# A fused attention and SwiGLU kernel: input transposed by the loading DMAs, or loaded plainly and turned on TensorE

## The chip, the cores and the metric

The kernel runs on one NeuronCore of a Trainium2 chip. The metric is the device time of one execution in microseconds (us), the median of several runs; before the change it is 844.42 us (three runs, 843.98 to 845.3). The profile shows one execution, whose span is 843.2 us.

The engines named below are TensorE (PE in the profile; its weight loads are PEld), VectorE (DVE), ScalarE (ACT), GpSimd (POOL) and SyncE (SP, which here only issues DMAs). Each runs its own instructions in order and waits on semaphores for the others.

## The reference

```python
x = A_x                                            # 1 x 2048 x 512, bf16
g = sigmoid((x * gate_w).sum(-1, keepdims=True))
qkv = (x @ A_wqkv).reshape(B, S, 3, 32, 16)        # 32 heads of 16
p = softmax(q @ k.T / sqrt(16))                    # 2048 x 2048 for each head
a = (p @ v, heads side by side) @ A_wo
b = (silu(x @ B_w_gate) * (x @ B_w_up)) @ B_w_down # 512 -> 1792 -> 512
out = g * a + (1 - g) * b
```

Every product needs x with its 512 features on the partitions, that is transposed: the tile `xT` of the kernel holds 4 blocks of 128 features (`dc`) by 2048 tokens.

## The kernel before

**The main loop.** Scores are made for a group of four heads (`g`, 8 of them), a quarter of 512 queries (`qb`, 4 of them) and a block of 128 keys. Most blocks get their exponential on ScalarE (tile `e_t`), the others get one that VectorE puts together from integer and float steps (tiles `y_t`, `z_t`, `u_t`, with one addition done by a DMA that GpSimd issues). A planner in the Python code simulates the engines and writes the order of TensorE, ScalarE and VectorE instructions by hand: `mm`, `act` and `vec` chain each instruction to the one before it on its engine (`ordered`, lines 145 to 168; most rows of the profile therefore carry L157, L160 or L166, and are told apart by their tiles). Projections, the FFN and the output products are put between the scores by the same planner. It starts counting after the start-up described next, so its order doesn't depend on it.

**The start-up.** Before the first scores the kernel needs K of head group 0 for all 2048 keys (written to `kaug[:, 0]`), Q of group 0 for the first 512 queries (`q0[0]`), and a bound that is subtracted ahead of the exponential: the largest magnitude of each row of K, times the magnitudes of Q.

- Lines 172 to 174: eight DMAs on SyncE's queue write `xT` through the transposing DMA, first the four feature blocks of the first 1024 tokens, then those of the second. ScalarE's queue loads the first 64 columns of the K, Q and V weights (lines 176 to 183). The remaining weights follow on SyncE's queue.
- Lines 211 to 236: VectorE writes constants, and spreads the K and Q weights of group 0 into zero-padded tiles (`wpad`, line 229), and presets three of the seven other groups of `kaug` with ones (`ones_rows`, line 234), a fourth one later (line 1013). GpSimd presets the last three and other tiles, and makes the identity matrix `ident` after them.
- Lines 992 to 1027: TensorE starts with 14 matmuls on zeros (`keep_warm`), then takes the feature blocks as they come: `k0(dc, tb)` adds one feature block to the K of a quarter of the tokens, in the PSUM tiles `kp0`; the Q of the first quarter goes to `qp0`. Two or three more `keep_warm` matmuls stand between the blocks. `v0` makes V of group 0 for eight token blocks.
- `largest` (a VectorE maximum over `kp0` into `kpart0`), small VectorE steps that turn it into the weights `kneg1` and `kneg0`, `k0_evict` (ScalarE, PSUM to `kaug[:, 0]`), ScalarE's copies of `qp0` to `q0r` and to `aq0` (magnitude), two masked VectorE copies from `q0r` to `q0[0]`, then the bound `bp0` and its addition to `q0[0]` close the start-up.

PSUM has eight banks here: two `kp0` tiles of two banks each (later the score tiles `s_t`), the three banks of `ps_m`, and the one of `ps_o`, where `keep_warm` writes.

Of the kernel before, what the change touches and what calls it, by code (L numbers as in the profile page):

```python
# [8 lines left out]
ACT = mybir.ActivationFunctionType  # L9
ALU = mybir.AluOpType  # L10
AX = mybir.AxisListType
BF16 = mybir.dt.bfloat16
F32 = mybir.dt.float32
# [65 lines left out]
def kernel(  # L79
# [12 lines left out]
    nc = tc.nc  # L92
    P = 128
    x = A_x.flatten_outer_dims()
    S, D = x.shape
    F = B_w_gate.shape[1]
    DH = 16
    H = D // DH
    G = H // 4
    NB = H // 8  # L100
    DC = D // P
    FC = F // P
    KT = S // P
    QBW = 512
    QB = S // QBW
    TQ = QBW // P
# [23 lines left out]
    const = ctx.enter_context(tc.tile_pool(name="const", bufs=1))  # L130
    big = ctx.enter_context(tc.tile_pool(name="big", bufs=1))
    work = ctx.enter_context(tc.tile_pool(name="work", bufs=2))
# [6 lines left out]
    ps_o = ctx.enter_context(tc.tile_pool(name="ps_o", bufs=1, space=bass.MemoryType.PSUM))  # L139
    ps_m = [ctx.enter_context(tc.tile_pool(name=f"ps_m{i}", bufs=1, space=bass.MemoryType.PSUM)) for i in range(3)]  # L140
# [4 lines left out]
    def ordered(ins):  # L145
        i = ins.ins
        if i.engine in last_of:
            tc.add_manual_dep(
                i, last_of[i.engine].name,
                mybir.DependencyInfo(mybir.DependencyClass.NoSync, mybir.DependencyReason.DATA),  # L150
                reason="order",
            )
        last_of[i.engine] = i
        return ins

    def mm(*args, **kw):
        return ordered(nc.tensor.matmul(*args, **kw))  # L157

    def act(*args, **kw):
        ordered(nc.scalar.activation(*args, **kw))  # L160
# [7 lines left out]
    vec = Ordered()  # L168


    xT = big.tile([P, DC, S], BF16, name="xT")
    for t0 in (0, 2 * QBW):
        for dc in range(DC):
            nc.sync.dma_start_transpose(out=xT[:, dc, t0:t0 + 2 * QBW], in_=x[t0:t0 + 2 * QBW, dc * P:(dc + 1) * P])
    wqk = big.tile([P, DC, 2 * D], BF16, name="wqk")
    for c0 in (D, 0):

        nc.scalar.dma_start(out=wqk[:, :, c0:c0 + 64],
                            in_=A_wqkv[:, c0:c0 + 64].rearrange("(dc p) c -> p dc c", p=P))

    rb = big.tile([P, NB, QBW], BF16, name="rb")
    wv = rb[:, :, :]
    nc.scalar.dma_start(out=wv[:, :, 0:64], in_=A_wqkv[:, 2 * D:2 * D + 64].rearrange("(dc p) c -> p dc c", p=P))

    nc.sync.dma_start(out=wv[:, :, 64:D], in_=A_wqkv[:, 2 * D + 64:3 * D].rearrange("(dc p) c -> p dc c", p=P))
    for c0 in (D, 0):
        nc.sync.dma_start(out=wqk[:, :, c0 + 64:c0 + D],
                          in_=A_wqkv[:, c0 + 64:c0 + D].rearrange("(dc p) c -> p dc c", p=P))
# [1 line left out]
    wo_t = big.tile([P, NB, D], BF16, name="wo_t")  # L190

    wo_l = big.tile([P, 2, D], BF16, name="wo_l")
    wd_t = big.tile([P, FC, D], BF16, name="wd_t")

    def late_loads():
        nc.sync.dma_start(out=gw_col[:], in_=gate_w.rearrange("(dc p) -> p dc", p=P))
# [9 lines left out]

    kaug = big.tile([P, G, S], BF16, name="kaug")

    mt = big.tile([P, FC, QBW], BF16, name="mt")
    idle = mt[:, 4, :]  # L210
    nc.vector.memset(idle, 0.0)
    wpad = [mt[:, i, :].rearrange("p (dc c) -> p dc c", c=P) for i in range(2)]
# [7 lines left out]
    vsel = const.tile([P, 2], F32, name="vsel")  # L220
# [3 lines left out]
    bsel0 = mt[:, 3, 0:P]  # L224
    nc.vector.memset(bsel0, 0.0)
    for j in range(4):
        nc.vector.memset(bsel0[32 * j:32 * j + 32, 32 * j:32 * j + 1], -1.0)
    for i in (1, 0):
        nc.vector.tensor_copy(
            out=wpad[i][:, :, :].rearrange("p dc (j c) -> p dc j c", c=32)[:, :, :, 1:1 + DH],  # L230
            in_=wqk[:, :, i * D:i * D + 64].rearrange("p dc (j c) -> p dc j c", c=DH))
    def ones_rows(engine, g):

        engine.memset(kaug[:, g, :].bitcast(F32), 1.0019378662109375)
    for g in range(1, 4):
        ones_rows(nc.vector, g)
    vaug = big.tile([P, KT, G * 4 * VC + 16], BF16, name="vaug")
    nc.gpsimd.memset(vaug[:, :, G * 4 * VC:], 0.0)

# [9 lines left out]
    for h in range(8):  # L249
        c = 2 * (h % 4) + h // 4  # L250
# [9 lines left out]
    nc.gpsimd.memset(sel_t[:], 0.0)  # L260
    for j in range(4):
        nc.gpsimd.memset(sel_t[32 * j:32 * j + 1, j:j + 1], 1.0)
    ident = const.tile([P, P], BF16, name="ident")
    nc.gpsimd.memset(ident[:], 1.0)
    nc.gpsimd.affine_select(out=ident[:], in_=ident[:], pattern=[[-1, P]], compare_op=ALU.is_equal,
                            fill=0.0, base=0, channel_multiplier=1)

    kb = const.tile([P, NB], F32, name="kb")
    kneg = const.tile([P, NB, 8], BF16, name="kneg")
# [74 lines left out]
    def m_free(ps, t):  # L344
        i = [h is ps for h in held].index(True)
        banks[i], held[i] = t + 0.2, None
# [96 lines left out]
    def v0(t0):  # L443

        p = m_tile("vp")
        for i in range(8):
            for dc in range(DC):
                mm(p[:, 64 * i:64 * i + 64], lhsT=xT[:, dc, (t0 + i) * P:(t0 + i + 1) * P], rhs=wv[:, dc, 0:64],
                   start=(dc == 0), stop=(dc == DC - 1))
        act(out=vaug[:, t0:t0 + 8, 0:4 * VC].rearrange("p t (h c) -> p t h c", c=VC)[:, :, :, 1:1 + DH],  # L450
            in_=p[:, :].rearrange("p (t h c) -> p t h c", h=4, c=DH), func=ACT.Copy)
        m_free(p, 0.0)
# [26 lines left out]
    q1 = big.tile([P, 2, QBW], BF16, name="q1")  # L479
    nc.gpsimd.memset(q1[:], 0.0)  # L480
    nc.gpsimd.memset(qx[0][:], 0.0)
    for g in range(5, G):
        ones_rows(nc.gpsimd, g)

    q0 = [(qx[1][:, :, :, :], on_t[0][:, :, :].rearrange("p (v i) q -> p v i q", v=2))[qb // 2][:, :, qb % 2, :]
          for qb in range(QB)]
# [479 lines left out]
    kp0 = [ps_s.tile([P, 2 * QBW], F32, tag="s", name="kp0") for _ in range(2)]  # L966
    qp0 = m_tile("qp0")
# [3 lines left out]
    def keep_warm(n):  # L971
        for _ in range(n):
            mm(warm[:, :], lhsT=idle[:, 0:P], rhs=idle[:, :], start=True, stop=True)

    def k0(dc, tb):
        mm(kp0[tb // 2][:, (tb % 2) * QBW:(tb % 2 + 1) * QBW], lhsT=wpad[1][:, dc, :],
           rhs=xT[:, dc, tb * QBW:(tb + 1) * QBW], start=(dc == 0), stop=(dc == DC - 1))

    kpart0 = const.tile([P, 3], F32, name="kpart0")
    aq0 = work.tile([P, QBW], BF16, tag="aq", name="aq0", bufs=4)  # L980
    q0r = work.tile([P, QBW], BF16, tag="qst", name="q0r")
    kneg0 = mt[:, 3, P:2 * P]
    kneg1 = mt[:, 3, 2 * P:3 * P]

    def largest(i, ps):
        vec.tensor_reduce(out=kpart0[:, i:i + 1], in_=ps, axis=AX.X, op=ALU.max, apply_absolute_value=True)

    def k0_evict(i):
        act(out=kaug[:, 0, i * 2 * QBW:(i + 1) * 2 * QBW], in_=kp0[i][:, :], func=ACT.Identity,
            bias=onescol[:, 0:1], scale=1.0)  # L990

    keep_warm(14)
    for dc in range(DC):
        for tb in range(2):
            k0(dc, tb)
        mm(qp0[:, :], lhsT=wpad[0][:, dc, :], rhs=xT[:, dc, 0:QBW], start=(dc == 0), stop=(dc == DC - 1))
        if dc < DC - 1:
            keep_warm(2)
    largest(0, kp0[0][:, :])
    act(out=q0r[:, :], in_=qp0[:, :], func=ACT.Copy)  # L1000
    act(out=aq0[:, :], in_=qp0[:, :], func=ACT.Abs)
    vec.tensor_scalar(out=kneg1, in0=bsel0, scalar1=kpart0[:, 0:1], scalar2=None, op0=ALU.mult)
    for v in range(2):
        vec.tensor_scalar(out=q0[0][:, v, :], in0=q0r[:, :], scalar1=vsel[:, v:v + 1], scalar2=None, op0=ALU.mult)
    k0_evict(0)
    for dc in range(DC - 1):
        for tb in (2, 3):
            k0(dc, tb)
        if dc == 0:
            v0(0)  # L1010
        else:
            keep_warm(3)
    ones_rows(vec, 4)
    k0(DC - 1, 2)
    largest(1, kp0[1][:, 0:QBW])
    vec.scalar_tensor_tensor(out=kneg0, in0=bsel0, scalar=kpart0[:, 1:2], in1=kneg1, op0=ALU.mult, op1=ALU.min)
    k0(DC - 1, 3)
    largest(2, kp0[1][:, QBW:2 * QBW])
    vec.scalar_tensor_tensor(out=kneg0, in0=bsel0, scalar=kpart0[:, 2:3], in1=kneg0, op0=ALU.mult, op1=ALU.min)
    k0_evict(1)  # L1020
    v0(8)
    bp0 = m_tile("bp0")
# [2 lines left out]
    for v in range(2):  # L1025
        vec.scalar_tensor_tensor(out=q0[0][:, v, :], in0=bp0[:, :], scalar=vsel[:, v:v + 1],
                                 in1=q0[0][:, v, :], op0=ALU.mult, op1=ALU.add)
# [3 lines left out]
                            op0=ALU.is_gt, op1=ALU.mult)  # L1031
    vec.scalar_tensor_tensor(out=bsel[:, :], in0=lo_t[:], scalar=0.5, in1=far_t[:],
                                   op0=ALU.is_lt, op1=ALU.mult)
# [15 lines left out]
    for qb in range(1, QB):  # L1049
        d = qb * KT  # L1050
# [5 lines left out]
    for qb in range(QB):  # L1056
        for b in range(NB):
            d = UNIT.index((qb, max(2 * b, 1))) * KT
# [31 lines left out]
    for qb in range(QB):  # L1090
        a0 = f0 + per * qb
        for fc in range(FC):
            load, pcs = gu[(qb, fc)]
            i = order_.index((qb, fc))
# [10 lines left out]
            c = pace.add(pcs, 58, a0 + per * (0.6 if qb < QB - 1 else 0.68) * (fc + 1) / FC, prev)  # L1105
            prev = [c]
        for tq in range(0, TQ, 2):
            c = pace.add(down_pieces(qb, tq), 0 if qb else 100, a0 + per * (0.6 + 0.3 * (tq + 2) / TQ if qb < QB - 1 else 0.68 + 0.32 * (tq + 2) / TQ), prev + fin_prev + gates)
# [191 lines left out]
    while au < UNITS:  # L1300
# [10 lines left out]
        if room > 0.02:  # L1311
# [6 lines left out]
            c = side(room + SLACK)  # L1318
# [9 lines left out]
            if room > 0.4 and closed in o_of and 0 < pvs[closed] < KT - 1 and sum(  # L1328
                    w for t, w in work_at[-24:] if t > plan.pe - 3.0) < 6.5:

                for j in range(4):
                    mm(o_of[closed][32 * j:32 * j + 16, :], lhsT=vaug[:, 0, G * 4 * VC:], rhs=xT[:, 0, 0:QBW],
                       start=False, stop=False, tile_position=(0, 32 * j), skip_group_check=True)
# [11 lines left out]
    while closed < UNITS or vops or added or vcur:  # L1345
# [9 lines left out]
        c = side(2.0)  # L1355
# [28 lines left out]
    for tq in range(TQ):  # L1384
        for j in range(4):
            mm(rps[32 * j:32 * j + 32, tq * P:(tq + 1) * P],
               lhsT=rt[:, 4 * tq + j:4 * tq + j + 1].broadcast_to([P, 32]), rhs=ident[:, :],
               start=True, stop=True, tile_position=(0, 32 * j), skip_group_check=True)
# [45 lines left out]
```

## Time and profile before

| | before |
|---|---|
| median time | 844.42 us |
| span of the profiled execution | 843.2 us |
| HBM read over the span | 20.83 MB |
| matmuls, `keep_warm` in the start-up | 26 |
| first matmul on `xT` | 6.68 us |
| last matmul of the start-up's K | 15.62 us |
| first exponential of the main loop | 18.83 us |

A row of the profile's timeline has the start in us from the beginning of the span, the duration in us, the engine, the line of the kernel, the operation, the tiles (output <- inputs), the shape, and how many instructions were merged into the row; in brackets stands how long the engine was idle before it and what released it. A row of the groups by shape ends with busy time and the mean duration of one in ns, then the idle time before them and its releasers. The table by stages has the stretch, its length, the busy time of PE, PEld, DVE, ACT and POOL with the number of instructions, the TensorE clock granted, the share of the DMA engines' time, and GB/s.

### The profile page before, as it was taken

To read this page: it belongs to the slowest core of one execution; us is meant where nothing else is said; L and a number is where in the kernel's file an instruction comes from. 1 tells how busy PE (TensorE), PEld (TensorE's weight loads), DVE (VectorE), ACT (ScalarE), POOL (GpSimd) and SP (SyncE) were. 2 spreads that over 40 slices of the span, in tenths; PEclk is the share of its full clock that TensorE was granted. 3 is DMA by queue.
4 is the path that set the end of the run, shared out by engine and by line. 5 is a ranking of instruction groups with operands and counts; after the bars stand their busy time and mean duration, and the time that the engine had idled before them with its cause. 6 is when DMAs were issued, how large, how long until landed. Compare 5 with 4: busy or idle time off the path is not lost. (4 is left out here: it accounts for less than half of the span.)

```text
span 843.2 us, 16224 instructions
## 1 busy us (share of the span) xinstructions
PE 763.7 (91%) x6047; PEld 263.8 (31%) x6076; DVE 795.7 (94%) x1159; ACT 815.1 (97%) x912; POOL 93.2 (11%) x122
## 2 busy tenths in 40 slices
PE   8999998999888998989889988899899898988997
PEld 3222233332332332222223323223333233332332
DVE  5999998999999999999999898999998999999996
ACT  3999999999999999999999999999999999999996
POOL 5010100010011010111010100100100110111000
PEclk9999999999999999999999999999999999999999
DMA  9432445245454334544443354454442464354232
GB/s 204 127 64 51 83 82 113 61 95 110 95 105 96 79 68 105 108 106 99 95 97 81 77 117 87 84 110 93 98 91 55 89 124 96 76 118 97 57 69 51
DMA packets 101416, 78.23 MB, mean 93 GB/s; under 512 B 77761, under 2 KB 89625, under 8 KB 101337
## 3 DMA queue, kind: packets, MB, share of 16 engines
q0 software_dynamic: 12672, 46.14, 28.7%
q1 hardware_dynamic: 86792, 30.60, 15.5%
q8 instruction: 47, 0.77, 0.4%
q10 hardware_dynamic: 1872, 0.46, 0.2%
q14 instruction: 33, 0.26, 0.1%
HBM read 20.83 MB, written 2.34 MB: 27 GB/s over the span
## 5 line engine op out<-in xcount | busy, mean ns | idle before, releaser
L160 ACT ACTIVATE e_t<-s_t 128x1024 bf16<-128x1024 f32 x846 | 791.9, 1103 | 8.2 <-PE s_t L157 6.2
L157 PE MATMUL s_t<-qx,kaug 64*128 64x512 bf16 x1376 | 293.8, 382 | 36.3 <-ACT e_t L160 31.2
L166 DVE TENSOR_SCALAR y_t<-d_t 128x512 uint16<-128x512 f32 x356 | 234.4, 680 | 16.4 <-PE d_t L157 13.5
L157 PEld LDWEIGHTS <-kaug 64*128 64x128 bf16 x2048 | 137.4, 93 | 324.1 <-issue 288.2
L157 PE MATMUL o_ps<-e_t,vaug 128*32 128x512 bf16 x1692 | 159.9, 389 | 1.5 <-DVE osb L166 1.0
L157 PE MATMUL gu_a<-xT,wg 64*128 64x512 bf16 x448 | 135.7, 377 | 0.0
L157 PE MATMUL gu_b<-xT,wu 64*128 64x512 bf16 x448 | 134.6, 377 | 1.2 <-DVE y_t L166 0.9
L157 PE MATMUL d_t<-qx,kaug 64*128 64x512 bf16 x288 | 107.6, 379 | 17.1 <-DVE y_t L166 10.3
L157 PEld LDWEIGHTS <-vaug 128*32 128x32 bf16 (+1 forms) x2132 | 45.6, 93 | 146.1 <-issue 144.8
L778 POOL DMA_DIRECT2D y_t<-u_t x44 | 40.1, 912 | 352.1 <-PE s_t L157 182.3
L778 POOL DMA_DIRECT2D y_t<-kaug x38 | 36.0, 946 | 309.7 <-PE s_t L157 199.7
L157 PE MATMUL dps_b<-wd_t,mt 64*128 64x512 bf16 x224 | 65.0, 375 | 0.3 <-DVE y_t L166 0.2
L157 PE MATMUL dps_a<-wd_t,mt 64*128 64x512 bf16 x224 | 64.9, 376 | 0.0
L166 DVE TENSOR_SCALAR z_t<-y_t 128x2048 uint16<-128x2048 uint16 x89 | 61.4, 690 | 2.1
L166 DVE TENSOR_SCALAR y_t<-y_t 128x2048 uint16<-128x2048 uint16 x89 | 60.8, 683 | 0.7 <-DMA y_t<-kaug 0.5
L166 DVE TENSOR_TENSOR u_t<-u_t 128x2048 f16<-128x2048 f16 x44 | 53.8, 1222 | 1.1
L166 DVE TENSOR_TENSOR u_t<-u_t,z_t 128x2048 f16<-128x2048 f16 x44 | 53.5, 1215 | 0.1
L157 PE MATMUL s_t<-q,kaug 64*128 64x512 bf16 x212 | 43.1, 381 | 7.6 <-ACT e_t L160 7.1
L166 DVE TENSOR_TENSOR kaug<-kaug 128x2048 f16<-128x2048 f16 x39 | 47.7, 1223 | 0.9
L157 PEld LDWEIGHTS <-wg 64*128 64x128 bf16 x448 | 41.3, 94 | 20.0 <-issue 7.7
L166 DVE TENSOR_TENSOR kaug<-kaug,z_t 128x2048 f16<-128x2048 f16 x39 | 47.4, 1216 | 0.1
L157 PEld LDWEIGHTS <-wu 64*128 64x128 bf16 x448 | 41.8, 94 | 14.7 <-issue 0.2
(131 smaller groups left out, 632.5 us busy)
## 6 DMA issues: line engine op xcount, KB each, us to landing
y_t<-u_t POOLq DMA_DIRECT2D x44, 512.0 KB, 4.8
y_t<-kaug POOLq DMA_DIRECT2D x38, 512.0 KB, 4.9
wg<-in_B_w_gate_dram SPq DMA_DIRECT2D x56, 128.0 KB
wu<-in_B_w_up_dram SPq DMA_DIRECT2D x56, 128.0 KB
y_t<-wd_t POOLq DMA_DIRECT2D x6, 512.0 KB, 4.6
on<-osb SPq DMA_DIRECT2D x120, 16.0 KB
rb<-rr SPq DMA_DIRECT2D x15, 128.0 KB
wd_t<-in_B_w_down_dram SPq DMA_DIRECT2D x7, 256.0 KB
```

What stands on the lines that cost most here:

```text
L157: return ordered(nc.tensor.matmul(*args, **kw))
L160: ordered(nc.scalar.activation(*args, **kw))
L166: return lambda *a, **kw: ordered(f(*a, **kw))
L778: nc.gpsimd.dma_start(out=ya, in_=ua, accum_op=ALU.add)
```

## The change

The input is loaded as it lies in HBM, a quarter of 512 tokens by each of four plain DMAs, into places that are free at that time: three quarters of the tile `wd_t` (the down-projection's weights come later) and a part of `mt`. TensorE turns it: a matmul with a 128x128 block of x as the weights and `ident` as the moving operand leaves the transposed block in PSUM. Four of them fill one bank (`tp`), which VectorE or ScalarE copies to `xT` (`turn`). Three banks take turns. The start-up is now ordered by quarters: turn the four feature blocks of the quarter, then its K, then its maximum.

With it go smaller edits. The padding of the weights moves from VectorE to ScalarE (`pad`), all seven presets of `kaug` go to GpSimd, whose identity matrix now comes first. The masked copies to `q0[0]` read `qp0` in PSUM, without `q0r`. The V columns for group 0 are loaded on SyncE's queue, between the second and third quarter of x. `kneg1` takes its minimum with a tile of zeros, in the form of instruction that the later steps have. `keep_warm` is left at the start alone, with 8 matmuls. The purpose is to load the input with plain descriptors, and to keep VectorE from copies within SBUF while GpSimd writes its presets.

```diff
     xT = big.tile([P, DC, S], BF16, name="xT")
-    for t0 in (0, 2 * QBW):
-        for dc in range(DC):
-            nc.sync.dma_start_transpose(out=xT[:, dc, t0:t0 + 2 * QBW], in_=x[t0:t0 + 2 * QBW, dc * P:(dc + 1) * P])
+    wd_t = big.tile([P, FC, D], BF16, name="wd_t")
+    mt = big.tile([P, FC, QBW], BF16, name="mt")
+    x_rows = [wd_t[:, TQ * b:TQ * b + TQ, :] for b in range(QB - 1)] + [mt[:, 8:8 + TQ, :]]
...
+    for b in range(QB):
+        nc.sync.dma_start(out=x_rows[b], in_=x[b * QBW:(b + 1) * QBW, :].rearrange("(i p) d -> p i d", p=P))
+        if b == 1:
+            nc.sync.dma_start(out=wv[:, :, 0:64],
+                              in_=A_wqkv[:, 2 * D:2 * D + 64].rearrange("(dc p) c -> p dc c", p=P))
...
-    for i in (1, 0):
-        nc.vector.tensor_copy(
-            out=wpad[i][:, :, :].rearrange("p dc (j c) -> p dc j c", c=32)[:, :, :, 1:1 + DH],
-            in_=wqk[:, :, i * D:i * D + 64].rearrange("p dc (j c) -> p dc j c", c=DH))
+    def pad(i):
+        act(out=wpad[i][:, :, :].rearrange("p dc (j c) -> p dc j c", c=32)[:, :, :, 1:1 + DH],
+            in_=wqk[:, :, i * D:i * D + 64].rearrange("p dc (j c) -> p dc j c", c=DH), func=ACT.Copy)
+    pad(1)
...
-    for g in range(1, 4):
-        ones_rows(nc.vector, g)
...
-    for g in range(5, G):
+    for g in range(1, G):
         ones_rows(nc.gpsimd, g)
...
-    keep_warm(14)
-    for dc in range(DC):
-        for tb in range(2):
-            k0(dc, tb)
-        mm(qp0[:, :], lhsT=wpad[0][:, dc, :], rhs=xT[:, dc, 0:QBW], start=(dc == 0), stop=(dc == DC - 1))
-        if dc < DC - 1:
-            keep_warm(2)
-    largest(0, kp0[0][:, :])
-    act(out=q0r[:, :], in_=qp0[:, :], func=ACT.Copy)
-    act(out=aq0[:, :], in_=qp0[:, :], func=ACT.Abs)
...
+    def turn(b, dc):
+        i = len(tps) % 3
+        tps.append((ps_m[1].tile([P, QBW], F32, tag="m1", name="tp") if i == 0 else
+                    ps_m[2].tile([P, QBW], F32, tag="m2", name="tp") if i == 1 else
+                    ps_o.tile([P, QBW], F32, tag="o", name="tp")))
+        tp = tps[-1]
+        for k in range(TQ):
+            mm(tp[:, k * P:(k + 1) * P], lhsT=x_rows[b][:, k, dc * P:(dc + 1) * P], rhs=ident[:, :],
+               start=True, stop=True)
+        dst = xT[:, dc, b * QBW:(b + 1) * QBW]
+        if dc % 2 or dc and b in (1, 2):
+            act(out=dst, in_=tp[:, :], func=ACT.Copy)
+        else:
+            vec.tensor_copy(out=dst, in_=tp[:, :])
+
+    keep_warm(8)
+    for b in range(QB):
+        for dc in range(DC):
+            turn(b, dc)
+        if b == 0:
+            pad(0)
+        if b == 2:
+            v0(0)
+        for dc in range(DC):
+            k0(dc, b)
+            if b == 0:
+                mm(qp0[:, :], lhsT=wpad[0][:, dc, :], rhs=xT[:, dc, 0:QBW], start=(dc == 0), stop=(dc == DC - 1))
+        if b == 0:
+            act(out=aq0[:, :], in_=qp0[:, :], func=ACT.Abs)
+            for v in range(2):
+                vec.tensor_scalar(out=q0[0][:, v, :], in0=qp0[:, :], scalar1=vsel[:, v:v + 1], scalar2=None, op0=ALU.mult)
+        elif b == 1:
+            largest(0, kp0[0][:, :])
+            vec.scalar_tensor_tensor(out=kneg1, in0=bsel0, scalar=kpart0[:, 0:1], in1=idle[:, 0:P],
+                                     op0=ALU.mult, op1=ALU.min)
+            k0_evict(0)
         else:
...
+            largest(b - 1, kp0[1][:, (b - 2) * QBW:(b - 1) * QBW])
+            vec.scalar_tensor_tensor(out=kneg0, in0=bsel0, scalar=kpart0[:, b - 1:b], in1=(kneg1, kneg0)[b - 2],
+                                     op0=ALU.mult, op1=ALU.min)
     k0_evict(1)
     v0(8)
```

More of the change, by code (lines that the diff above doesn't have):

```diff
@@ L171 @@
     xT = big.tile([P, DC, S], BF16, name="xT")
-    for t0 in (0, 2 * QBW):
-        for dc in range(DC):
-            nc.sync.dma_start_transpose(out=xT[:, dc, t0:t0 + 2 * QBW], in_=x[t0:t0 + 2 * QBW, dc * P:(dc + 1) * P])
+    wd_t = big.tile([P, FC, D], BF16, name="wd_t")
+    mt = big.tile([P, FC, QBW], BF16, name="mt")
+    x_rows = [wd_t[:, TQ * b:TQ * b + TQ, :] for b in range(QB - 1)] + [mt[:, 8:8 + TQ, :]]
+    rb = big.tile([P, NB, QBW], BF16, name="rb")
+    wv = rb[:, :, :]
+    for b in range(QB):
[3 more added lines that the diff above has]
+                              in_=A_wqkv[:, 2 * D:2 * D + 64].rearrange("(dc p) c -> p dc c", p=P))
     wqk = big.tile([P, DC, 2 * D], BF16, name="wqk")
@@ L179 @@
                             in_=A_wqkv[:, c0:c0 + 64].rearrange("(dc p) c -> p dc c", p=P))
-    rb = big.tile([P, NB, QBW], BF16, name="rb")
-    wv = rb[:, :, :]
-    nc.scalar.dma_start(out=wv[:, :, 0:64], in_=A_wqkv[:, 2 * D:2 * D + 64].rearrange("(dc p) c -> p dc c", p=P))
     nc.sync.dma_start(out=wv[:, :, 64:D], in_=A_wqkv[:, 2 * D + 64:3 * D].rearrange("(dc p) c -> p dc c", p=P))
@@ L192 @@
     wo_l = big.tile([P, 2, D], BF16, name="wo_l")
-    wd_t = big.tile([P, FC, D], BF16, name="wd_t")
     def late_loads():
@@ L207 @@
     kaug = big.tile([P, G, S], BF16, name="kaug")
-    mt = big.tile([P, FC, QBW], BF16, name="mt")
     idle = mt[:, 4, :]
@@ L227 @@
         nc.vector.memset(bsel0[32 * j:32 * j + 32, 32 * j:32 * j + 1], -1.0)
-    for i in (1, 0):
-        nc.vector.tensor_copy(
-            out=wpad[i][:, :, :].rearrange("p dc (j c) -> p dc j c", c=32)[:, :, :, 1:1 + DH],
-            in_=wqk[:, :, i * D:i * D + 64].rearrange("p dc (j c) -> p dc j c", c=DH))
+    def pad(i):
+        act(out=wpad[i][:, :, :].rearrange("p dc (j c) -> p dc j c", c=32)[:, :, :, 1:1 + DH],
+            in_=wqk[:, :, i * D:i * D + 64].rearrange("p dc (j c) -> p dc j c", c=DH), func=ACT.Copy)
+    pad(1)
     def ones_rows(engine, g):
         engine.memset(kaug[:, g, :].bitcast(F32), 1.0019378662109375)
-    for g in range(1, 4):
-        ones_rows(nc.vector, g)
+    ident = const.tile([P, P], BF16, name="ident")
+    nc.gpsimd.memset(ident[:], 1.0)
+    nc.gpsimd.affine_select(out=ident[:], in_=ident[:], pattern=[[-1, P]], compare_op=ALU.is_equal,
+                            fill=0.0, base=0, channel_multiplier=1)
     vaug = big.tile([P, KT, G * 4 * VC + 16], BF16, name="vaug")
@@ L262 @@
         nc.gpsimd.memset(sel_t[32 * j:32 * j + 1, j:j + 1], 1.0)
[L263 to L266, printed above, removed]
     kb = const.tile([P, NB], F32, name="kb")
@@ L980 @@
     aq0 = work.tile([P, QBW], BF16, tag="aq", name="aq0", bufs=4)
-    q0r = work.tile([P, QBW], BF16, tag="qst", name="q0r")
     kneg0 = mt[:, 3, P:2 * P]
@@ L990, in k0_evict @@
             bias=onescol[:, 0:1], scale=1.0)
-    keep_warm(14)
-    for dc in range(DC):
-        for tb in range(2):
-            k0(dc, tb)
-        mm(qp0[:, :], lhsT=wpad[0][:, dc, :], rhs=xT[:, dc, 0:QBW], start=(dc == 0), stop=(dc == DC - 1))
-        if dc < DC - 1:
-            keep_warm(2)
-    largest(0, kp0[0][:, :])
-    act(out=q0r[:, :], in_=qp0[:, :], func=ACT.Copy)
-    act(out=aq0[:, :], in_=qp0[:, :], func=ACT.Abs)
-    vec.tensor_scalar(out=kneg1, in0=bsel0, scalar1=kpart0[:, 0:1], scalar2=None, op0=ALU.mult)
@@ L1003 @@
[L1003 to L1009, printed above, removed]
-            v0(0)
-        else:
[L1012 to L1016, printed above, removed]
@@ L1017 @@
-    k0(DC - 1, 3)
-    largest(2, kp0[1][:, QBW:2 * QBW])
-    vec.scalar_tensor_tensor(out=kneg0, in0=bsel0, scalar=kpart0[:, 2:3], in1=kneg0, op0=ALU.mult, op1=ALU.min)
+    tps = []
+    def turn(b, dc):
[12 more added lines that the diff above has]
+            vec.tensor_copy(out=dst, in_=tp[:, :])
```

## The prediction

> **What bounds the kernel now.** I read the page first: parts 1 and 5 say that ScalarE's exponentials fill the span.
>
> ```profile
> PE 763.7 (91%) x6047; PEld 263.8 (31%) x6076; DVE 795.7 (94%) x1159; ACT 815.1 (97%) x912; POOL 93.2 (11%) x122
> ...
> L160 ACT ACTIVATE e_t<-s_t 128x1024 bf16<-128x1024 f32 x846 | 791.9, 1103 | 8.2 <-PE s_t L157 6.2
> ```
>
> 846 exponentials keep ScalarE busy; it idles only 8.2 us before them. So the time is the moment of the first exponential plus a stretch that hardly has holes. The change works ahead of that moment only: comparing the lists of instructions of the two built programs, with names stripped of their numbers, every engine has the same order after the first scores. The question is therefore when the first exponential starts. The timeline of the first 24 us answers for before:
>
> ```profile
> 0.81 11.24 SPq L174 DMA_TRANSPOSE xT<-in_A_x_dram  x8
> ...
> 14.46 0.38 PE L157 MATMUL kp<-xT,mt 128*128 128x512 bf16 x1
> ...
> 14.88 0.69 DVE L166 TENSOR_REDUCE kpart<-kp 128x1 f32<-128x512 f32 x1 [1.22 <-PE kp L157]
> ...
> 16.03 0.69 DVE L166 TENSOR_REDUCE kpart<-kp 128x1 f32<-128x512 f32 x1
> 16.76 1.11 ACT L160 ACTIVATE kaug<-kp,onescol 128x1024 bf16<-128x1024 f32 x1 [3.35 <-DVE kpart L166]
> ...
> 17.77 0.59 ACT L160 ACTIVATE vaug<-vp 128x512 bf16<-128x512 f32 x1
> ...
> 18.83 2.98 ACT L160 ACTIVATE e_t<-s_t 128x1024 bf16<-128x1024 f32 x3 [0.47 <-PE s_t L157]
> ...
> 23.34 13.36 ACT L160 ACTIVATE e_t<-s_t 128x1024 bf16<-128x1024 f32 x14 [1.53 <-PE s_t L157]
> ```
>
> The eight transposing loads are issued over 11.24 us, and the K projection of the last quarter can start its last step only at 14.46. Then a serial tail: maximum, small scale, next projection, maximum (ends 16.03 + 0.69 = 16.72), K eviction, V eviction, first score, exponential at 18.83. From the last maximum to the exponential: 18.83 - 16.72 = 2.11 us. After 23.34 the exponentials stand 13.36 / 14 = 0.954 us apart, without a hole.
>
> The table by stages shows what the loads move:
>
> ```profile
> 2.00:5.00 3.00, 3.00 (x8) 1.06 (x7) 0.89 (x11) 1.28 (x1) 3.00 (x13) 1.00 1.17 171
> 5.00:10.00 5.00, 5.00 (x22) 2.20 (x21) 2.99 (x4) 0.00 (x0) 4.66 (x13) 1.00 1.16 212
> 10.00:15.00 5.00, 4.66 (x48) 2.40 (x48) 3.04 (x6) 2.65 (x4) 1.90 (x3) 1.00 1.06 192
> 15.00:20.00 5.00, 3.02 (x40) 1.75 (x41) 3.85 (x9) 2.77 (x4) 0.00 (x0) 1.00 1.04 330
> ```
>
> The last column is GB/s: with the DMA engines full, transposing loads get 171 to 212, the plain loads after them (15 to 20 us) 330. That is what the change can win. It pays with copies out of PSUM, whose rows by shape are:
>
> ```profile
> L166 DVE CAST osb<-o_ps 128x512 bf16<-128x512 f32 x32 | 21.8, 682 | 2.2 <-PE o_ps L157 2.0
> ...
> L160 ACT ACTIVATE q0r<-qp 128x512 bf16<-128x512 f32 x1 | 0.6, 597 | 7.1 <-PE qp L157 7.1
> ...
> L166 DVE TENSOR_SCALAR qx<-qp,vsel 128x512 bf16<-128x512 f32 x2 | 1.4, 744 | 0.9 <-PE qp L157 0.9
> ```
>
> Back to back they stand closer than their durations: 0.66 us on VectorE (two in 1.34), 0.50 to 0.55 on ScalarE (10.76, 11.26, 11.81), 0.70 for a masked copy (two in 1.41).
>
> [...] the first warming matmuls stand 0.427 us apart, the later ones 0.216, from about 6.1 us on[...]. [...] TensorE idles 1.64 us ahead of 22.38 and stays warm. [...] the K eviction above waits 3.35 us, until the maximum that reads the same tile is done. [...]
>
> **The change, part by part.**
>
> Loads. 2.1 MB at 330 GB/s takes 6.4 us; traffic begins about 2.0 us in before. Quarters land at roughly 4, 6, 7.5 and 9 us, with the small weight loads between. Bound for the first: 0.52 MB at 330 gives 3.6, at 171 with the weights' 0.13 MB gives 5.8. I take up to 4.7, where the 8 warming matmuls end (1.25 + 8 x 0.427 = 4.67), so that it costs nothing. From there on the loads are ahead.
>
> Turning. Per quarter: 16 matmuls of N = 128 in 4 groups, each group a PSUM bank and a copy of 128x512 to SBUF. Three banks rotate, so the fourth group waits for the first copy. Only then the quarter's K projection can finish, then its maximum. All engines work in order, and what is queued behind decides. Worked through, times in us:
>
> - Quarter 0: [...] the fourth waits for VectorE's copy (5.3 to 5.96), is copied by ScalarE until 7.05. The Q padding, now behind it on ScalarE, takes 0.35 (SBUF copy of 256 elements, estimated from VectorE's 0.30): 7.4. Seven more projections at 0.216 and 0.38 for the last: 9.2. The magnitude on ScalarE, 0.58: 9.8. VectorE's two masked copies wait for it (same bank): 2 x 0.70, 11.25.
> - Quarter 1: its first copy is queued on VectorE behind these: 11.9. Its fourth group waited for that bank: 12.4; ScalarE's copy 13.0; last projection 13.4; maximum over 1024, 1.22: 14.65.
> - Quarter 2: VectorE does the small scale (0.30) before its copy: 15.65. ScalarE's K eviction waits for the maximum, 14.75 to 15.8, with three copies queued behind it: 17.45. The fourth group's bank came free at 15.65 and the V projection runs meanwhile. Last projection 18.35; maximum 0.69, scale 0.35: 19.45.
> - Quarter 3: copy 20.1, fourth group 20.6, ScalarE's copy 21.2, projection 21.6, maximum until 22.35.
> - Tail unchanged, 2.11: exponential at 24.45, against 18.83: **5.6 later**.
>
> Warming. 14 + 12 warming matmuls become 8. None was on the path after 6.7 us except as filler; nothing gained.
>
> Wait added on ScalarE. The table load now stands behind the wait of the first padding for its weights, so it runs after about 3.6 us (when before's padding could start), to 4.9[...]. [...] I take 0.3.
>
> Presets. VectorE's four presets of kaug (0.91 each) go to GpSimd, which then has 7 x 0.95 = 6.65 us and is done near 16.5, before any use; first users are DMAs of a later stage. Nothing. The weights for later stages load sooner; nothing waited for them. Removing the copy q0r saves 0.5 on ScalarE, paid by two masked copies from PSUM (1.41 instead of 0.61), counted above.
>
> Sum: 5.6 + 0.3 = 5.9, and 844.42 + 5.9 = **850.3**.
>
> **The rivals.**
>
> 1. Forecast: the chain of copies and in-order queues replaces the DMA as the bound of the start. 850.3.
> 2. Copies overlap so well that the start follows the loads: last quarter lands at 9, then one quarter's turning, copies and projection (about 2.3), and from its maximum to the exponential 0.69 + 2.11: 14.1, 4.7 earlier: **839.7**. For it: the DMA really was full until 14.5. Against it: 16 copies, 3 maxima and the masked copies stand in an alternating chain, and VectorE's masked copies sit ahead of quarter 1's.
> 3. TensorE's clock comes late or falls back, with no warming matmuls between the quarters. Warm only at 9.5[...]: 1.2 more, **851.5**. Cold through the whole start: 5 to 6 more, **856**. For it: gaps of 1 to 2 us in each quarter. Against it: before kept warm over 1.64.
> 4. Later holes swallow the delay: **844.4**. For it: ScalarE idles 1.53 before 23.34. Against it: that hole belongs to the chain behind the first scores, which keeps its order and moves along.
>
> **How the numbers follow.** Case 1: 0.72; case 2: 0.08; case 3: 0.16, half of it the mild form; case 4: 0.04. Case 1 alone spans 847.5 (copies pipelining better than my chain, 2.8 less) to 852.5 (late first load, 1.1[...]). The range adds most of case 3: 847.5 to 854, leaving out cases 2 and 4 and the cold half of 3, two in ten. Faster 0.08, same 0.04, slower 0.88.
>
> **What would show it.** Right: first exponential near 24.5 to 25; the transposed groups' fourth matmul waiting on VectorE's tp copies; ScalarE's first kaug eviction waiting on kpart; loads landed by 10 us; exponentials unchanged in number and spacing. Wrong: the last kpart maximum before 18 us (case 2), [...] or a first exponential at 24.5 with an unchanged time (case 4).

## The result and the profile after

The changed kernel takes 855.15 us (median of four runs, 854.0 to 855.93), the kernel before 844.86 in the same comparison: ratio 1.0118, 95% interval 1.0097 to 1.0139. That is 10.3 us slower, where 5.9 was forecast and the range ended at 854.0.

The exponentials kept their number and nearly their idle time (8.2 us before), as this row of the groups by shape of the changed kernel shows:

```profile
L160 ACT ACTIVATE e_t<-s_t 128x1024 bf16<-128x1024 f32 x846 | 793.3, 1122 | 9.0 <-PE s_t L157 7.7 <-PE d_t L157 0.3
```

The loss lies ahead of them. The timeline of the changed kernel's start:

```profile
5.57 0.84 PE L157 MATMUL tp<-ident,wd_t 128*128 128x128 bf16 x12 [0.72 <-DMA wd_t<-in_A_x_dram]
5.78 1.28 ACT L160 ACT_TABLE_LOAD   x1 [5.78 <-DMA wqk<-in_A_wqkv_dram]
...
8.86 0.61 PE L157 MATMUL qp<-xT,mt 128*128 128x512 bf16 x1 [0.89 <-ACT mt L160]
...
11.39 0.63 PE L157 MATMUL qp<-xT,mt 128*128 128x512 bf16 x1
...
14.75 0.38 PE L157 MATMUL tp<-ident,wd_t 128*128 128x128 bf16 x4 [1.87 <-DVE xT L166]
...
17.49 1.11 ACT L160 ACTIVATE kaug<-kp,onescol 128x1024 bf16<-128x1024 f32 x1 [1.72 <-DVE kpart L166]
...
19.14 1.87 PE L157 MATMUL vp<-rb,xT 128*128 128x64 bf16 x32 [0.26 <-ACT xT L160]
...
20.82 1.86 PE L157 MATMUL kp<-xT,mt 128*128 128x512 bf16 x4
...
25.94 0.69 DVE L166 TENSOR_REDUCE kpart<-kp 128x1 f32<-128x512 f32 x1 [0.94 <-PE kp L157]
...
28.74 2.98 ACT L160 ACTIVATE e_t<-s_t 128x1024 bf16<-128x1024 f32 x3 [0.47 <-PE s_t L157]
```

The first exponential starts at 28.74 us instead of 18.83: 9.9 later, and the medians differ by 10.3. The waits named in the prediction are there: the fourth group of a quarter waits for VectorE's copy (14.75), and the K eviction for the maximum (17.49). From the last maximum's end (25.94 + 0.69) to the exponential it is 2.11 us, as before. New are the long matmuls: 0.63 us for the projection at 11.39, where before had 0.38, and 1.87 us for the 32 small V matmuls, where before had 1.09. The table by stages tells why; its last column but two is the TensorE clock granted:

```profile
9.00:10.00 1.00, 1.00 (x3) 0.30 (x2) 0.00 (x0) 0.00 (x0) 1.00 (x2) 0.50 1.10 350
...
11.00:12.00 1.00, 1.00 (x5) 0.45 (x4) 0.00 (x0) 0.00 (x0) 1.00 (x3) 0.50 1.09 376
...
13.00:14.00 1.00, 0.00 (x0) 0.00 (x0) 1.00 (x2) 0.78 (x2) 1.00 (x2) 1.00 1.09 369
...
20.00:22.00 2.00, 2.00 (x22) 1.26 (x20) 0.00 (x0) 0.66 (x2) 0.00 (x0) 0.50 0.93 212
```

TensorE ran at half clock from about 8.9 to 12.3 us and again from about 19.1 to 22.5. The ends are worked out from the slices with a mixed clock: 0.94 in the one from 8 to 9 us, 0.86 from 12 to 13, 0.78 from 18 to 20 and 0.87 from 22 to 24.

The plain loads did move more. From 5 to 10 us, when both kernels load x, the changed kernel's slices average 285 GB/s against 212 before. The 350 to 376 above are for the last of x and, by an estimate from the bytes moved, from about 10.4 us on for the weights queued behind it.

### The profile page after: what moved, and what is told of

It reads as the page before. It is cut to its first block, busy times and chain, and to the rows that moved or that the text cites. A ratio compares the mean times of both kernels' runs of the same rounds, so it can differ in the third digit from the quotient of the medians.

```text
span 854.2 us, 16367 instructions
## 1 busy us (share of the span) xinstructions
PE 773.3 (91%) x6122; PEld 266.7 (31%) x6122; DVE 796.5 (93%) x1159; ACT 821.0 (96%) x923; POOL 96.9 (11%) x126
```

## The experiments

First the summary; "start" is the first exponential of the main loop in the profiled run. In the profiled executions, what comes after the start takes 823.5 to 825.6 us of the span in all ten kernels, so a difference in start is a difference in time to about a microsecond either way. The medians of e2 and e6 lie some 2 us higher than their starts say: their profiled executions were among the quicker ones.

| kernel | start, us | time, us | ratio to before, 95% interval |
|---|---|---|---|
| before | 18.83 | 844.86 to 845.25 | 1 |
| after | 28.74 | 855.15 | 1.0118 (1.0097 to 1.0139) |
| e1_warm | 25.26 | 850.78 | 1.0066 (1.0044 to 1.0088) |
| e2_table | 26.23 | 854.35 | 1.0108 (1.0083 to 1.0132) |
| e3_warm_table | 25.30 | 850.74 | 1.0069 (1.0046 to 1.0093) |
| e4_no_turn | 19.73 | 845.46 | 1.0007 (0.9997 to 1.0017) |
| e5_masks_late | 23.50 | 849.44 | 1.0045 (1.0024 to 1.0065) |
| e6_pipelined | 22.31 | 850.44 | 1.0061 (1.0040 to 1.0083) |
| e7_half | 19.05 | 846.04 | 1.0012 (0.9995 to 1.0028) |
| e8_half2 | 16.77 | 842.02 | 0.9961 (0.9948 to 0.9974) |

### e1_warm: fill TensorE's waits

```diff
+        spare = kp0[1][:, 0:QBW] if b < 2 else qp0[:, :]
         for dc in range(DC):
+            if dc == 3 and b:
+                keep_warm((0, 7, 7, 4)[b], spare)
             turn(b, dc)
         if b == 0:
             pad(0)
+            keep_warm(1, spare)
...
             k0(dc, b)
+            if b == 0 and dc == 0:
+                keep_warm(2, spare)
```

> The changed kernel with 21 matmuls on zeros put into TensorE's waits between the turning matmuls (into PSUM banks that are free then), so that it doesn't pause for long. Theory A (the copies' chain delays the start by the forecast amount, and TensorE's clock, at half speed from 8.9 to 12.4 us and from 19 to 22.5 us, adds 2.9 us on top of it): no stretch at half clock after 6 us, last maximum ends near 23.8 instead of 26.63 us, first exponential near 25.8 instead of 28.74 us, time 2.9 us below the changed kernel's, about 852.3. Rival B (TensorE waits for copies anyway, so its clock is hidden): first exponential stays within 0.5 us of 28.7, time as the changed kernel's, about 855.

The start moved to 25.26 us, 3.5 sooner, and the time fell by 4.4 us. Its timeline, then a stretch of its table by stages:

```profile
8.46 0.39 PE L157 MATMUL qp<-xT,mt 128*128 128x512 bf16 x1 [0.46 <-ACT mt L160]
...
9.76 0.38 PE L157 MATMUL qp<-xT,mt 128*128 128x512 bf16 x1
...
17.26 1.09 PE L157 MATMUL vp<-rb,xT 128*128 128x64 bf16 x32 [0.26 <-ACT xT L160]
18.19 1.03 PE L157 MATMUL kp<-xT,mt 128*128 128x512 bf16 x4
```

```profile
8.00:10.00 2.00, 1.54 (x9) 0.72 (x9) 0.00 (x0) 0.40 (x2) 2.00 (x2) 1.00 1.09 348
```

From the first Q projection to the end of the last it is 1.68 us here (8.46 to 10.14), 3.16 in after (8.86 to 12.02). From the start of the V matmuls to the end of K of the third quarter it is 1.96 (17.26 to 19.22) against 3.54 (19.14 to 22.68). The two differences, 1.5 and 1.6, make 3.1 of the 3.5; the other 0.4 is the first load, which landed at 5.17 in this run and at 5.57 in after's. All slices of e1 from 4 to 26 us have the full clock. Theory A holds (2.9 expected, 3.1 measured), B falls: work that was added made the kernel faster. With the waits filled, the work on the path kept a granted clock of 1.00, where after had 0.50.

### e2_table and e3_warm_table: the table load out of the way

```diff
+    first_act = const.tile([P, 1], F32, name="first_act")
+    act(out=first_act[:], in_=onescol[:], func=ACT.Copy)
     pad(1)
```

> The changed kernel with one tiny activation ahead of the first padding, so that ScalarE's table load no longer stands behind the wait for the K weights. Theory A: the load runs at about 2 us, ScalarE's first copies of turned blocks move from 7.41 to about 6.2 us, the Q padding ends near 8.0 instead of 8.80 us, and the first exponential comes 0.8 us sooner (0.4 to 1.2, as the clock's steps may shift), near 27.9. Rival C (the table load is hidden behind VectorE's copy and the loads): first exponential within 0.2 us of 28.74.

> Both edits together: matmuls on zeros in TensorE's waits, and the table load early. What stays is the chain of copies and in-order queues alone, with the first load landing at 5.6 us. Theory A: first exponential near 25.0 us, which is the forecast's chain (24.45) plus the 0.9 us by which the first load lands later than assumed, less a little; time about 851.5, 3.7 us below the changed kernel's. Rival B: the chain itself was underestimated, and the first exponential stays above 27 us.

With this edit alone the table load ran at 1.95 us and ScalarE's first copies at 6.41. The median fell by the 0.8 us that theory A had, which is less than the two intervals can tell apart, while the profiled execution started 2.5 us sooner, since its clock fell for one stretch only in the start:

```profile
14.00:16.00 2.00, 2.00 (x12) 1.22 (x11) 0.68 (x1) 0.21 (x1) 1.48 (x2) 0.50 1.14 304
```

So e2 can't size the table load: the half-clock stretches moved with it. The granted clock also differs between executions of one kernel: e2's four fall into two pairs, 853.1 us with a mean granted clock of 0.991 and 855.5 with 0.986. With the clock held up (1.00 in all its slices from 4 to 26 us), e3 can size it: 25.30 against e1's 25.26, and 850.74 against 850.78. The first load landed 0.17 later there than in e1, so the early table load is worth 0.1 us at most. Something else takes its place, as e3's timeline shows:

```profile
7.99 0.45 ACT L160 ACTIVATE mt<-wqk 128x256 bf16<-128x256 bf16 x1 [0.45 <-DMA wqk<-in_A_wqkv_dram]
```

The Q padding (tile `mt` from `wqk`) now waits for its 64 KB of weights, which land near 8 us beside the plain loads of x; in e1 it started at 7.96. Theory A's 25.0 for e3 was close; its reason for the 0.8 in e2 isn't shown.

### e4_no_turn: undo the turning alone

```diff
-    for b in range(QB):
-        nc.sync.dma_start(out=x_rows[b], in_=x[b * QBW:(b + 1) * QBW, :].rearrange("(i p) d -> p i d", p=P))
...
+    for t0 in (0, 2 * QBW):
+        for dc in range(DC):
+            nc.sync.dma_start_transpose(out=xT[:, dc, t0:t0 + 2 * QBW], in_=x[t0:t0 + 2 * QBW, dc * P:(dc + 1) * P])
...
-        for dc in range(DC):
-            turn(b, dc)
...
+            if b in (0, 2) and dc < DC - 1:
+                keep_warm(3)
```

> The changed kernel with only its loads undone: the eight transposing DMAs and the V columns on ScalarE's queue as before, no turning matmuls and no copies to xT; padding on ScalarE, presets on GpSimd, masked copies from PSUM and the order by quarters stay; matmuls on zeros fill the waits for the loads as before. Theory A (the turning and its copies are the whole loss): first exponential near 19.4 us, 0.6 later than before's 18.83 because the last quarter's K waits for the maximum of the quarter ahead in the same PSUM tile; time about 845.4. Rival D (presets on GpSimd, padding on ScalarE or the order by quarters cost several us themselves): first exponential above 21 us, time above 847.

845.46 us; the interval, 0.9997 to 1.0017, holds before's time. Presets on GpSimd, padding on ScalarE, masked copies from PSUM and the order by quarters together cost 0.9 us of start. Most of it is what was forecast, as the timeline of before and then that of e4 show:

```profile
15.62 0.38 PE L157 MATMUL kp<-xT,mt 128*128 128x512 bf16 x1 [0.78 <-DVE kpart L166]
```

```profile
15.87 1.02 PE L157 MATMUL kp<-xT,mt 128*128 128x512 bf16 x4 [0.78 <-DVE kpart L166]
...
19.73 2.98 ACT L160 ACTIVATE e_t<-s_t 128x1024 bf16<-128x1024 f32 x3 [0.47 <-PE s_t L157]
```

The wait for the maximum is in both, 0.78 us. But before has only one K step of the last quarter behind it, and e4 has all four, 0.65 us more at 0.216 each. The other 0.25 is there ahead of the wait, 15.87 against 15.62. Rival D falls: about 9 of the 9.9 us belong to turning x, its copies and the clock.

### e5_masks_late: a copy nobody waits for yet

```diff
-            for v in range(2):
-                vec.tensor_scalar(out=q0[0][:, v, :], in0=qp0[:, :], scalar1=vsel[:, v:v + 1], scalar2=None, op0=ALU.mult)
         elif b == 1:
+            for v in range(2):
+                vec.tensor_scalar(out=q0[0][:, v, :], in0=qp0[:, :], scalar1=vsel[:, v:v + 1], scalar2=None, op0=ALU.mult)
             largest(0, kp0[0][:, :])
```

On top of e3, and with one matmul on zeros in that wait instead of seven.

> The kernel with matmuls on zeros in the waits and the table load early, and one more edit: the two masked copies to q0 stand behind quarter 1's first copy on VectorE instead of ahead of it (six fewer matmuls on zeros in the wait that this removes). Theory A (in-order queues set the chain: a copy that somebody waits for stands behind copies that nobody waits for yet): quarter 1's maximum starts near 12.8 instead of 14.38 us, the first exponential comes 1.4 to 1.5 us sooner, near 23.8 instead of 25.30, time about 849.2. Rival E (ScalarE's copies of the same quarter end last anyway): first exponential within 0.3 us of 25.3.

```profile
10.28 0.69 DVE L166 CAST xT<-tp 128x512 bf16<-128x512 f32 x1 [2.91 <-PE tp L157]
...
10.89 1.40 DVE L166 TENSOR_SCALAR qx<-qp,vsel 128x512 bf16<-128x512 f32 x2
...
12.58 1.23 DVE L166 TENSOR_REDUCE kpart<-kp 128x1 f32<-128x1024 f32 x1 [0.30 <-PE kp L157]
```

In this timeline the quarter's copy goes first (10.28), and the masked copies hide behind ScalarE's. The maximum starts at 12.58 instead of 14.38, the first exponential at 23.50 instead of 25.30; the medians differ by 1.3 us. Theory A holds with 0.3 us to spare. To have two masked copies of 1.4 us together stand ahead of one that is waited for had cost 1.8 us.

### e6_pipelined: turn everything, in another order

```diff
+    turns(0)
+    turns(1)
+    pad(0)
+    kk(0)
+    turns(2)
+    kk(1)
+    largest(0, kp0[0][:, :])
...
+    turns(3)
+    kk(2)
...
+    kk(3)
...
+    largest(1, kp0[1][:, :])
```

Here `turns(b)` is the four groups of a quarter and `kk(b)` its K; copies alternate between the engines.

> All of x still loaded plainly and turned, table load early, but the queues in another order: a quarter is turned before the K of the quarter ahead of it, copies alternate between VectorE and ScalarE, the second half's two maxima become one over 1024 columns, the Q projection and the masked copies come last. Theory A (order, not the amount of copying, is the loss): VectorE has about 9.7 us and ScalarE about 8.5 us of work from 5.5 us on; worked through, the last maximum ends near 16 and the first exponential starts near 18.6 us, so the time is about that of before, 844.5 (843.5 to 846). Rival F (16 copies, their waits and the clock can't be packed that well): first exponential above 21 us, time above 847.

A miss for A: 22.31 us and 850.44. Its timeline:

```profile
14.43 0.38 PE L157 MATMUL tp<-ident,mt 128*128 128x128 bf16 x4 [1.64 <-DVE xT L166]
...
17.44 1.23 DVE L166 TENSOR_REDUCE kpart<-kp 128x1 f32<-128x1024 f32 x1 [2.47 <-PE kp L157]
...
20.43 0.39 PE L157 MATMUL bp<-aq,mt 128*128 128x512 bf16 x1 [1.16 <-DVE qx L166]
```

The last quarter's group waits 1.64 for a copy queued behind the first maximum, VectorE then idles 2.47, and the bound waits 1.16 for the masked copies, whose PSUM bank it reuses. So the orders tried by hand, this one and e5's, failed to pack the start. Whether turning all of x could match before stays open. The kernel had no fillers within the start, and the clock was at half from 21.4 us (0.86 in the slice from 20 to 22, 0.50 from 22 to 24) to about 24.8: the four projections at 22.95 took 1.89 us, the two scores at 24.77 took 0.41. Its seven executions range from 847.95 us at a mean granted clock of 0.996 to 853.4 at 0.986. Before's own in the same comparison range from 843.17 at 0.999 to 849.59 at 0.987, so this spread isn't the start's alone.

### e7_half and e8_half2: share the work

The first 1024 tokens are loaded plainly and turned, the others come through four transposing DMAs behind them.

```diff
+        if b < 2:
+            nc.sync.dma_start(out=x_rows[b], in_=x[b * QBW:(b + 1) * QBW, :].rearrange("(i p) d -> p i d", p=P))
+        else:
+            for dc in (2 * b - 4, 2 * b - 3):
+                nc.sync.dma_start_transpose(out=xT[:, dc, 2 * QBW:], in_=x[2 * QBW:, dc * P:(dc + 1) * P])
```

> Half and half: the first 1024 tokens loaded plainly and turned (8 groups, copies alternate between VectorE and ScalarE), the last 1024 by four transposing DMAs that follow on the same queue; table load early, one maximum for each half. Theory A (before is bound by the transposing DMAs at 171 to 212 GB/s, after by copies, so sharing the work shortens both): loads done near 11.7 us instead of 14.4, last maximum ends near 13.6, first exponential near 15.8 instead of 18.83 us, time about 3 us below before's, 841.8. Rival F: copies still hold the chain, first exponential above 19 us, time as before's or above.

Start 19.05 and 846.04: not told apart from before, and 3 us later than theory A said. The timeline of e7 shows what stood between its K steps:

```profile
11.90 1.10 PE L157 MATMUL vp<-rb,xT 128*128 128x64 bf16 x32
12.83 0.60 PE L157 MATMUL kp<-xT,mt 128*128 128x512 bf16 x2
...
13.79 0.59 PE L157 MATMUL qp<-mt 128*128 128x512 bf16 x2 [0.36 <-DVE qx L166]
14.22 0.59 PE L157 MATMUL kp<-xT,mt 128*128 128x512 bf16 x2
14.65 0.59 PE L157 MATMUL qp<-mt 128*128 128x512 bf16 x2
...
15.72 1.23 DVE L166 TENSOR_REDUCE kpart<-kp 128x1 f32<-128x1024 f32 x1 [1.98 <-PE kp L157]
```

The first fillers (matmuls on zeros, here `qp<-mt`) wrote into the bank that the masked copies were still reading, and K stood behind them. That wait is only about 0.5 us: the two K steps from 12.83 stream for 0.43, and the filler starts at 13.79. The expectation of e8 counts 0.96 from the start of these steps. The V matmuls ahead of K took 0.93 (11.90 to 12.83), and the four fillers 0.86 by themselves at 0.216 each. e8 takes all three out:

```diff
-        if dc == 0:
-            v0(0)
-        elif dc < DC - 1:
-            keep_warm(2, qp0[:, :])
+    v0(0)
...
-        vec.tensor_scalar(out=q0[0][:, v, :], in0=qp0[:, :], scalar1=vsel[:, v:v + 1], scalar2=None, op0=ALU.mult)
+        act(out=q0[0][:, v, :], in_=qp0[:, :], func=ACT.Identity, scale=vsel[:, v:v + 1])
```

> The half-and-half kernel again, with what held it up taken out: no matmuls on zeros in the second half (two of them waited 0.96 us for VectorE's masked copies, whose bank they write), the first V projection behind the last K step, and the two masked copies on ScalarE. Theory A (nothing but these waits kept it at 19.05 us): the transposing loads are in by about 12.5 us, the last K step ends near 13.4, the one maximum starts there instead of at 15.72, and the first exponential comes near 17.1 us, 1.7 ahead of before's 18.83; time about 843.3. Rival G (the transposing loads behind the plain ones land no sooner than 14 us): maximum after 14.7, first exponential 18.3 or later, time within 1 us of before's.

```profile
11.51 1.89 PE L157 MATMUL kp<-xT,mt 128*128 128x512 bf16 x8
...
13.44 1.23 DVE L166 TENSOR_REDUCE kpart<-kp 128x1 f32<-128x1024 f32 x1 [0.98 <-PE kp L157]
...
16.77 3.07 ACT L160 ACTIVATE e_t<-s_t 128x1024 bf16<-128x1024 f32 x3 [0.31 <-PE s_t L157]
```

The eight K steps of the second half run back to back from 11.51, so the transposing loads are in by then or nearly so, and one maximum follows, 2.28 us sooner than in e7; the three shares above make 2.3. Theory A holds, rival G falls. The start is 16.77 us, 2.06 ahead of before's, and the time 842.02 us: faster than both kernels. The medians gain 3.2 us. The profiled spans gain 2.8 (843.2 to 840.4), 0.7 of it after the start and within the 2 us by which that part varies.

Not all of the 2.06 need come from sharing the work. e8 also has one maximum for the second half where before has two, one after the other. With before's own times, the last quarter's K step could follow the one at 14.46 after 0.216 us, at 14.68; its maximum could start 0.42 later, as the one at 14.88 does, and one of 1.22 us over both quarters would end at about 16.3 instead of 16.72. By this estimate 0.4 us may belong to the single maximum; no run separates the two.

## Why the prediction was right or wrong

**What bounds the kernel: right.** The start sets the time, as the ten spans above show. One reading of before was off: the K step at 14.46 is the third quarter's last, and the last quarter's stands at 15.62. The sum takes its tail from the maximum's end, so nothing rests on it.

**The chain of copies: right in mechanism and size.** The forecast had 24.75 us for the first exponential, 0.3 of it for the table load, with the first turning at 4.67. In e1, where the clock holds, turning begins at 5.17, so 0.5 later, and the exponential comes at 25.26, 0.5 later. The parts agree too: from the end of the Q projections to the end of the last maximum the forecast has 13.15 us (9.2 to 22.35) and e1 13.02 (10.14 to 23.16). The two readers of a bank that go one after the other (in after, ScalarE's magnitude from 12.06 to 12.66 us, then VectorE's masked copies at 12.69), the masked copies ahead of quarter 1's copy (e5, 1.8 us) and the fourth group behind VectorE's copy (1.87 us ahead of 14.75) are all in the trace.

**The clock: the step that failed.** The sum prices every matmul after quarter 0's groups at the full clock, 0.216 for a projection, and leaves a fall of the clock to rival 3, at 0.16. In after the clock fell twice, and that cost 3.1 us (against e1). It wasn't rival 3's mild form, a clock that comes only at 9.5 us (my estimate, a time that no trace shows) for 1.2 us: TensorE was at full clock by the first turning (the twelve matmuls at 5.57 took 0.84 us, as many at 16.04 with a granted clock of 1.00 took 0.83) and lost it later. With the first load 0.9 later than assumed, the sum closes: 24.75 + 0.9 + 3.1 = 28.75, against 28.74 measured.

The reason against rival 3 was "before kept warm over 1.64", a gap taken as the measure. In after the longest wait, 1.87 us ahead of 14.75, brought no fall, while shorter ones did. Each fall in after lasted 3.4 us (8.9 to 12.3 and 19.1 to 22.5), as did the one in the start of e2 (12.9 to 16.3, from its slices at 0.73, 0.50 and 0.92) and, to about 0.1, the one in e6 (21.4 to about 24.8). So I took TensorE's busy time, from the profile, in the 3.4 us ahead of each fall: 1.66 us (5.5 to 8.9) and 1.51 (15.7 to 19.1) in after, about 1.4 in e2 and about 1.6 in e6. In e1 every slice of 2 us from 4 to 24 us has 1.42 us or more of work, and its clock never fell there. But after has 1.53 us of work from 12.3 to 15.7, and before 1.65 from 19.0 to 22.4, and the clock was full behind both. So the falls came behind stretches with little work, in after not behind its longest pause. What sets them off isn't shown: no run varied the work alone in small steps.

**The first load: undersized.** Assumed in by 4.7, at most 5.8; it came at 5.17 to 5.57, 0.5 to 0.9 on the path.

**Table load and padding: right sum, wrong reason.** The 0.3 was my estimate; the traces show no more than the 1.28 us of the load itself. In after it ends at 7.06 and the padding starts at 7.08. What was on the path is the late arrival of the small weights: the K weights released the table load at 5.78 us, where the forecast had 3.6, and e3 waits for the Q weights until 7.99. Presets and padding elsewhere cost nothing that shows, as forecast (e4).

**The range.** It left out the cold half of rival 3; a rival that the forecast's own idle stretches speak for had a better claim than one in six. The upper end of case 1, 852.5, is also more than its terms give: 850.3 + 1.1 for the first load is 851.4; the rest was my estimate, which no trace shows.

## What to carry to other kernels

When a change thins out TensorE's work, ask how busy each few microseconds leave it. Here the clock fell to half for 3.4 us at a time (after, e2), for all of TensorE's work in that time. Cheap matmuls into a free bank paid for themselves where TensorE waited anyway (e1, a start 3.5 us sooner), but not ahead of work that was ready (0.86 us in e7), nor into a bank that somebody still read (about 0.5 us in e7). A change of who transposes moved the bound from the DMA to the copies out of PSUM; where each alone was too slow (starts at 18.83 and 28.74 us), half on each was best of the kernels run (16.77, e8). In queues that run in order, put the copy that another engine waits for ahead of the one that is needed later (1.8 us in e5).

## What the runs showed of the hardware

A plain load of 512 KB issued at 0.81 us could be used at 5.17 to 5.57 us. The 64 KB of Q weights, in rows of 128 bytes, came at about 8.0 us beside the plain loads (e3, where the padding waits for them until 7.99), and at about 5.4 beside the transposing ones (e4, where it waits until 5.42). What makes the difference isn't shown.
